# A seven-product form, used twice, for the last tile's up stage

## The chip, the cores and the metric

The kernel runs on one core of a Trainium2 chip. Its time is the device time of one execution in microseconds, the median of several runs. A core has five engines that run their own instruction queues and wait for each other through semaphores: PE (matmuls), DVE (vector work), ACT (activations, copies), POOL (element-wise work, no access to PSUM) and SP (here only a queue that issues DMA transfers). PE reads its operands from SBUF, the on-chip memory, and leaves results in banks of PSUM; a bank holds 512 float32 values in each of 128 partitions.

## What is computed

A retention layer over 8 batches, 8 heads, 576 positions and a head size of 64 makes `x`, 4608 tokens of 512 features. A gated feed-forward block follows; it is the larger part of the work and the one that the change touches. All is float32.

```python
def _moe_ref(x, w_gate, w_val, w_out) -> np.ndarray:
    g = x @ w_gate
    silu = g * (1.0 / (1.0 + np.exp(-g)))
    val = x @ w_val
    return (silu * val @ w_out).astype(np.float32)
...
    x = np.ascontiguousarray(attn_out.transpose(0, 2, 1, 3)).reshape(B * S, H * D)
    return _moe_ref(x=x, **moe_kwargs)
```

`w_gate` and `w_val` are 512 by 1536, `w_out` is 1536 by 512.

## The kernel before

**Tiles.** The tokens go in five tiles: tile 0 has 512 tokens and plain matmuls, tiles 1 to 4 have 1024 each. Each of these has an up stage (gate and value products, then Silu and a multiply) and a down stage (product with `w_out`). While tile n is computed, the retention layer for tile n+1 runs in pieces between its steps (`tick`); for tile 4 all of it is done within tile 3's stages.

**Fewer products.** The matrices of a stage are cut into blocks, and a fast scheme (the tables `UP` and `DOWN`, 26 lines each) makes the block results from 26 products of sums of blocks, where the plain form would need 32. A line of `UP` gives the label of a PSUM bank, whether the product opens the bank or adds onto what is there, the slot of the input sum with the sums that make it, the slot of the weight sum with its sums, and what is done with the product. The 1536 hidden columns are taken as three quads (`qd`, `NQ = 3`) of four 128-row blocks, gate and value side by side. So an up stage has 3 x 26 = 78 steps (`up_step`), each with four matmul calls of 128 by 128 by 256 (line 1124); a down stage has 26 steps (`down_step`) with six (line 1173). A step's products are used by `reads`: ACT copies a bank (line 1058), DVE adds bank and SBUF, POOL adds two SBUF tiles (line 1061), ACT applies Silu (line 1145) and DVE or POOL multiplies (lines 1148, 1152).

**Sums of weights.** They do not depend on the tile. They are made once: for the up stage during tile 1 (POOL and ACT), where each operand that PE uses is also written to DRAM (`up_ops`, by ACT's DMA queue), and for the down stage during tile 0 (`dn_ops`). From tile 2 on a step's operand is one load from DRAM, issued by SP, into a ring of eight slots of 768 columns (`fetch`, line 1022; `operand`). `fetch` is called after each step and loads what is needed eight steps on. The loads of the retention inputs (lines 306 to 317) and the stores of results (line 1182) go through the same SP queue, in program order.

**Sums of inputs.** A tile's input sums (`x_sums`, line 910) are made on DVE in the last steps of the down stage before it and on POOL during its first quad; the sums of hidden blocks for a down stage (also line 910) on DVE and POOL within its steps.

**Order.** The program order of each engine's queue is that of the source; `merge` spreads the retention pieces evenly over the steps of a stage. Nothing reorders it later. The instructions of an engine run in that order, each when its semaphores allow.

Of the kernel before, what the change touches and what calls it, by code (L numbers as in the profile page):

```python
# [12 lines left out]
F32 = mybir.dt.float32  # L13
# [4 lines left out]
ALU = mybir.AluOpType  # L18
# [117 lines left out]

def terms(text):

    return [t.split() for t in text.split(",") if t.strip()]
# [16 lines left out]
def kernel(  # L156
# [83 lines left out]
    ring = arena[:, 4 * QW + 2560 - 8 * 768 :].rearrange("p (s x) -> p s x", x=768)  # L240
# [672 lines left out]
    dn_ops = [dr.tile([P, 768], F32, name=f"dn{i}") for i in range(N)]  # L913

# [96 lines left out]
    fetches = [("dn", 1, i) for i in range(N)]  # L1011
    for n in range(2, NTILE):
        fetches += [("up", qd, i) for qd in range(NQ) for i in range(N)] + [("dn", n, i) for i in range(N)]
    fetched = [0]
    turn = [5, 4, 1, 6, 7, 2, 0, 3]

    def fetch():
        m = fetched[0]
        if m < len(fetches):
            what, a, i = fetches[m]  # L1020
            src = up_ops[a][i] if what == "up" else dn_ops[i]
            nc.sync.dma_start(out=ring[:, turn[m % 8], 0 : src.shape[-1]], in_=src)
            fetched[0] += 1

    used = [0]

    def operand():
        m = used[0]
        used[0] += 1
        return ring[:, turn[m % 8]]  # L1030
# [77 lines left out]
    def up_step(n, qd, i):  # L1108
# [5 lines left out]
        if busy:  # L1114
            if i > 1:
                w_sums(qd, i)
            w = up_view(qd)(wslot)
        else:
            w = operand()[:, 0:512].rearrange("p (g x) -> p g x", g=2)
# [7 lines left out]
        if busy:  # L1127
            nc.scalar.dma_start(out=up_ops[qd][i].rearrange("p (g x) -> p g x", g=2), in_=w)
            if i in (20, 23) and qd + 1 < NQ:
                first_sums(qd + 1, *((0, 2) if i == 20 else (2, 4)))  # L1130
# [5 lines left out]
            if qd + 1 == NQ:  # L1136
                for _ in range({21: 3, 22: 2, N - 1: 3}.get(i, 0)):
                    fetch()
# [23 lines left out]
    def down_step(n, i):  # L1162
        label, opens, slot, hops, ops = down[i]
        for op in hops:
            add(nc.gpsimd if i % 3 == 1 and op[0] != "nad" else nc.vector, op, hid_view)
        w = operand().rearrange("p (q x) -> p q x", q=NQ)
# [30 lines left out]
        if 0 <= at < X_FIRST and n + 1 < NTILE:  # L1197
            x_sums(n + 1, at, at + 2, True)
        go_on(3)


# [91 lines left out]
    for n in range(1, NTILE):  # L1293
        upto = needed(n + 1) if n + 1 < NTILE else done
        cut = (done + upto + (n == 1) * 2) // 2
        ups = [lambda qd=qd, i=i: up_step(n, qd, i) for qd in range(NQ) for i in range(N)]
# [49 lines left out]
```

## Time and profile before

| what | value |
|---|---|
| median of 3 runs | 1044.39 us (1042.32 to 1045.34) |
| span of the profiled execution, first to last instruction | 1037.2 us, 21564 instructions |
| mean clock granted to PE | 0.998 |
| busy in the last tile's up stage, 831.5 to 966.2 (134.7 us) | PE 134.7, DVE 56.8, ACT 34.4, POOL 49.7 |
| busy in the down stage before it, 762 to 831 (69 us) | PE 68.9, DVE 44.3, ACT 6.3, POOL 26.4 |
| busy in tile 3's up stage, 629 to 762 (133 us) | PE 133.0, DVE 62.0, ACT 33.7, POOL 45.0 |
| DMA over the span | 199.12 MB, 192 GB/s |
| operand loads of up stages | 234, 256 KB each, 2.6 us from issue to landing (median) |
| operand loads of down stages | 104, 384 KB each, 3.8 us |

The profile comes from one execution and has its own span, which begins with the first instruction and ends with the last; the device time of a run has more around it. Busy times of different engines overlap. An engine that is busy all the time sets the length of a stage; one that isn't can still do so, where another waits for it. A matmul call of float32 shows as two records of 128 by 256.

### The profile page before, as it was taken

To read this page: it belongs to the slowest core of one execution; us is meant where nothing else is said; L and a number is where in the kernel's file an instruction comes from. 1 tells how busy PE (TensorE), PEld (TensorE's weight loads), DVE (VectorE), ACT (ScalarE), POOL (GpSimd) and SP (SyncE) were. 2 spreads that over 40 slices of the span, in tenths; PEclk is the share of its full clock that TensorE was granted. 3 is DMA by queue.
4 is the path that set the end of the run, shared out by engine and by line. 5 is a ranking of instruction groups with operands and counts; after the bars stand their busy time and mean duration, and the time that the engine had idled before them with its cause. 6 is when DMAs were issued, how large, how long until landed. Compare 5 with 4: busy or idle time off the path is not lost.

```text
span 1037.2 us, 21564 instructions
## 1 busy us (share of the span) xinstructions
PE 1023.1 (99%) x8440; PEld 846.0 (82%) x8440; DVE 633.2 (61%) x1070; ACT 299.6 (29%) x653; POOL 419.9 (40%) x369
## 2 busy tenths in 40 slices
PE   6999999999999999999999999999999999999998
PEld 5654555888888888888888888888888888888887
DVE  4488878676768667446458685435465644344644
ACT  3566433253544222222322103223211022231110
POOL 3401265867564236522134057222242583222425
PEclk9999999999999999999999999999999999999999
DMA  9999877777679887674686686555554465555653
GB/s 240 258 279 263 200 218 269 204 205 191 196 194 265 211 244 220 177 197 133 188 231 173 176 208 208 153 142 153 159 171 148 143 196 153 153 153 160 182 163 100
DMA packets 307244, 199.12 MB, mean 192 GB/s; under 512 B 215944, under 2 KB 251784, under 8 KB 307144
## 3 DMA queue, kind: packets, MB, share of 16 engines
q1 hardware_dynamic: 275720, 161.17, 58.2%
q10 hardware_dynamic: 30784, 36.18, 10.4%
q8 instruction: 67, 1.10, 0.5%
q0 software_dynamic: 640, 0.39, 0.2%
q14 instruction: 33, 0.27, 0.1%
HBM read 157.58 MB, written 40.11 MB: 191 GB/s over the span
## 4 chain that ended last, share of the span: by engine, by line
PE 93%; DMA 3%; DVE 1%; ACT 1%; issue 1%; SPq 1%; POOL 0%; DVEq 0%; ACTq 0%; POOLq 0%
PE bankC L1124 13%; PE bankE L1124 13%; PE bankB L1124 13%; PE bankA L1124 13%; PE bankB L1173 7%; PE bankC L1173 7%; PE bankE L1173 7%; PE bankA L1173 7%; PE outer L556 2%; PE bankA L877 2%; PE bankB L877 1%; PE bankE L877 1%; PE outer L583 1%; PE inner L597 1%; PE inner L567 1%; PE bankC L877 1%
## 5 line engine op out<-in xcount | busy, mean ns | idle before, releaser
L1061 POOL TENSOR_TENSOR rest<-rest 128x512 f32<-128x512 f32 x65 | 91.7, 1415 | 234.3 <-DVE rest L1061 212.8
L1145 ACT ACTIVATE io<-rest 128x256 f32<-128x256 f32 x180 | 75.0, 416 | 305.4 <-DVE rest L1061 262.4
L1124 PE MATMUL bankC<-rest,arena 128*128 128x256 f32 x544 | 129.0, 380 | 0.0
L1124 PE MATMUL bankA<-rest,arena 128*128 128x256 f32 x544 | 128.7, 379 | 0.0
L910 POOL TENSOR_TENSOR arena<-arena 128x512 f32<-128x512 f32 (+1 forms) x72 | 110.6, 1549 | 37.3 <-DMA up<-arena 26.5
L1124 PE MATMUL bankB<-rest,arena 128*128 128x256 f32 x512 | 121.2, 380 | 0.5 <-DMA arena<-up 0.5
L1124 PE MATMUL bankE<-rest,arena 128*128 128x256 f32 x512 | 121.4, 380 | 0.1
L1152 POOL TENSOR_TENSOR arena<-rest,io 128x256 f32<-128x256 f32 x72 | 51.9, 726 | 167.7 <-ACT io L1145 167.7
L1124 PEld LDWEIGHTS bankA<-rest,arena 128*128 128x128 f32 x544 | 103.2, 190 | 14.5 <-issue 0.5
L1124 PEld LDWEIGHTS bankC<-rest,arena 128*128 128x128 f32 x544 | 102.9, 190 | 14.4 <-POOL arena L910 0.3
L1124 PEld LDWEIGHTS bankB<-rest,arena 128*128 128x128 f32 x512 | 97.0, 190 | 14.0 <-issue 0.8
L1124 PEld LDWEIGHTS bankE<-rest,arena 128*128 128x128 f32 x512 | 97.0, 190 | 13.7 <-DVE rest L1061 0.5
L910 POOL TENSOR_TENSOR rest<-rest 128x256 f32<-128x256 f32 (+1 forms) x69 | 68.9, 1020 | 71.8 <-DMA dn<-rest 35.3
L1061 DVE TENSOR_TENSOR rest<-bankB,rest 128x512 f32<-128x512 f32 x72 | 48.9, 687 | 67.1 <-PE bankB L1124 52.5
L1061 DVE TENSOR_TENSOR rest<-bankC,rest 128x512 f32<-128x512 f32 x72 | 48.9, 687 | 65.5 <-PE bankC L1124 46.9
L1061 DVE TENSOR_TENSOR rest<-bankA,rest 128x512 f32<-128x512 f32 x72 | 48.9, 687 | 61.2 <-PE bankA L1124 45.1
L1061 DVE TENSOR_TENSOR rest<-bankE,rest 128x512 f32<-128x512 f32 x71 | 48.2, 687 | 60.5 <-PE bankE L1124 47.1
L1148 DVE SCALAR_TENSOR_TENSOR arena<-rest,io 128x256 f32<-128x256 f32 x84 | 56.7, 676 | 10.8 <-ACT io L1145 10.8
L1173 PE MATMUL bankC<-arena 128*128 128x256 f32 x252 | 58.3, 380 | 0.1
L1173 PE MATMUL bankB<-arena 128*128 128x256 f32 x252 | 58.2, 381 | 0.0
L1173 PE MATMUL bankA<-arena 128*128 128x256 f32 x252 | 57.9, 379 | 0.0
L1173 PE MATMUL bankE<-arena 128*128 128x256 f32 x252 | 57.9, 379 | 0.0
(204 smaller groups left out, 1626.1 us busy)
## 6 DMA issues: line engine op xcount, KB each, us to landing
arena<-up SPq DMA_DIRECT2D x234, 256.0 KB, 2.6
arena<-dn SPq DMA_DIRECT2D x104, 384.0 KB, 3.8
up<-arena ACTq DMA_DIRECT2D x78, 256.0 KB, 3.7
dn<-rest SPq DMA_DIRECT2D x78, 128.0 KB, 1.8
out_dram<-rest SPq DMA_DIRECT2D x31, 256.0 KB, 3.9
qk<-in_q_dram SPq DMA_DIRECT2D x108, 72.0 KB, 2.6
qk<-in_k_dram SPq DMA_DIRECT2D x108, 72.0 KB, 2.7
rest<-in_moe_w_out_dram ACTq DMA_DIRECT2D x6, 1024.0 KB
```

The lines of the kernel that those rows point to most:

```text
L556: m = nc.tensor.matmul(value(i, hl, c), s["v"][rows, at], ret[rows, c % 2 if whole(i) else hl, c // 2], start=start, stop=start, skip_grou ...
L567: nc.tensor.matmul(z[half[hl], r, c], s["kn"][chunk(i, hl, 2 * c + r)], s["v"][rows, at], start=True, stop=True, skip_group_check=True)
L583: nc.tensor.matmul(xr[half[hl]] if c + 1 == NC else value(i, hl, c), state[half[hl], c, :], s["qT"][half[hl], ts(c, L)], start=False, stop ...
L597: nc.tensor.matmul(sc[chunk(i, hl, 2 * c + r)[0], r if whole(i) else hl, c], kT[half[hl], at], qT[half[hl], at], start=True, stop=True, sk ...
L877: nc.tensor.matmul(bank, w, xs[0][:, c, :], start=(c == 0), stop=(c == HP - 1))
L910: eng.tensor_tensor(out=dst, in0=srcs[0], in1=srcs[1], op=ALU.add if op[0] == "add" else ALU.subtract)
L1061: eng.tensor_tensor(out=at(op[1]), in0=at(op[2]), in1=at(op[3]), op=ALU.add if op[0] == "add" else ALU.subtract)
L1124: m = nc.tensor.matmul(b[:, gv * TB : (gv + 1) * TB], w[:, gv, ts(c, P)], rhs[:, c, :], start=(opens and gv == 0 and c == 0), stop=(c == 1 ...
L1145: nc.scalar.activation(out=s, in_=src[:, 0:TB], func=AF.Silu, scale=-1.0 if negative else 1.0)
L1148: return lambda: nc.vector.scalar_tensor_tensor(out=dst, in0=src[:, TB : 2 * TB], scalar=-1.0, in1=s, op0=ALU.mult, op1=ALU.mult)
L1152: nc.gpsimd.tensor_tensor(out=dst, in0=src[:, TB : 2 * TB], in1=s, op=ALU.mult)
L1173: nc.tensor.matmul(b[:, m * TB : (m + 1) * TB], lhs[:, qd, ts(m, P)], w[:, qd], start=(opens and qd == 0 and m == 0), stop=(qd == NQ - 1), ...
```

## The change

Only tile 4's up stage (`FINE = (4,)`) gets another scheme; tiles 1 to 3 keep `UP`. The product of a 2 by 2 block matrix by another is made from seven products and sums (the form with four sums on each side and seven afterwards). It is applied twice: seven outer products, in the order `FINE_ORDER = (1, 2, 6, 7, 4, 5, 3)`, each of which is itself made from seven inner products. An inner product is two matmul calls (gate and value), 128 by 128 by 256. With three quads there are 3 x 7 = 21 turns of seven inner products.

```python
        def product(k, i):
            ...
            b = bank_of(k, i)
            opens = i in (1, 2, 5)
            for g in range(2):
                nc.tensor.matmul(b[:, g * TB : (g + 1) * TB], w[:, g], x(o, i),
                                 start=(opens and g == 0), stop=True, skip_group_check=True)
```

Inner products 1, 6, 7 and 4 add onto each other in one bank (of four that take turns, `chain_banks`), and ACT copies what is there after each of the first three; 5 and 3 share a second bank, 2 has a third. The order within a turn, with what is issued to ACT and DVE, is written out. `k` is the turn, `r` the place in it; the fourth product of turn k-1 comes in turn k:

```python
        def step(k, r):
            own, last = 0 <= k < K, 0 < k
            t = temps(k)
            if own and r == 0:
                product(k, 1)
                nc.scalar.copy(out=t["p1"], in_=bank_of(k, 1))
            if own and r == 1:
                product(k, 5)
                nc.scalar.copy(out=t["p5"], in_=bank_of(k, 5))
            if last and r == 2:
                product(k - 1, 4)
                used[0] += 1
                fetch()
            if own and r == 3:
                product(k, 6)
                nc.scalar.copy(out=t["u2"], in_=bank_of(k, 6))
            if own and r == 4:
                product(k, 2)
            if own and r == 5:
                product(k, 3)
            if own and r == 6:
                product(k, 7)
                nc.scalar.copy(out=t["u3"], in_=bank_of(k, 7))
            if late and own:
                for _ in range(2):
                    if late:
                        late.pop(0)()
            if r == 0 and last:
                done(k - 1, 12)
            if r == 1 and last:
                before = temps(k - 1)
                made(k - 1, 22, before["u3"], before["p5"])
                done(k - 1, 22)
            if r == 2 and last:
                if seq[k - 1][1] == 1:
                    nc.scalar.copy(out=held[spot[21]], in_=bank_of(k - 1, 4))
                else:
                    onto(k - 1, 21, bank_of(k - 1, 4))
            if r == 3 and last:
                done(k - 1, 21)
            if own and r == 4:
                made(k, 11, bank_of(k, 2), t["p1"])
            if own and r == 5:
                made(k, 12, bank_of(k, 3), t["u2"])
            if own and r == 6:
                done(k, 11)
```

`made` is one DVE sum of 128 by 512 for one of the four inner results (11, 12, 21, 22), with one input from PSUM for 11 and 12; the result 21 is what stands in the chain's bank after product 4. `onto` adds the result to the running outer sums, also on DVE, and `finish` (called by `done` for the outer products 2, 4, 5 and 3, after which a hidden block is complete) is a Silu on ACT and a multiply on POOL:

```python
        def onto(k, c, src):

            o = seq[k][1]
            r, at = held[spot[c]], temps(k)[home[c]]
            if o == 2 or o == 3:
                combine(nc.vector, at, src, r, 1)
            elif o == 6:
                combine(nc.vector, r, src, r, 1)
            elif o == 7:
                combine(nc.vector, kept(k, c), src, r, 1)
            elif o == 4:
                combine(nc.vector, at, src, kept(k, c), 1)
            elif o == 5:
                combine(nc.vector, r, src, r, 1)
                combine(nc.vector, at, src, kept(k, c), 1)
```

The temporaries are three sets that take turns; `kept` lies in the hidden rows of the next quad. In outer product 1 `made` writes the running sums themselves, and there is no `onto`.

**Sums of inputs.** For tile 4 four outer sums of 128 by 1024 go to DVE in steps 18 to 21 of tile 3's down stage, in place of eight of 128 by 512 in steps 21 to 24; the inner sums of 128 by 256 are on POOL: 8 for outer products 1 and 2 in steps 21 to 24, 20 more (`late`) two at each place from the first turn on.

**Sums of weights.** Their 49 combinations for each quad are made in six rounds, one for each quad and side (gate or value), from eight blocks of 128 by 256. Five of the blocks are in `up_ops` already; the other three are written to DRAM by ACT's queue during tile 1's up stage (`w_raw`, after steps 2, 6 and 10 of each quad). A round loads eight blocks with SP, turns the sign of one on ACT, makes four outer sums of 128 by 512, eight inner sums of 128 by 256 and four of 128 by 384, and stores the results to `fine_ops` in DRAM with 14 or 15 transfers on SP. The rounds lie here (stage, quad, side; V is DVE, G is POOL):

```python
        def up_round(n, stage, qd, g, at):
            load, turned, outer, z4, z3, store4, store3 = weight_round(qd, g, place_up(stage), (G, V, G) if stage else (V, V, V))
            for d, blocks in enumerate(((4, 6), (0, 2), (5, 7), (1, 3))):
                put(n, stage, at + d, lambda blocks=blocks: load(*blocks))
            put(n, stage, at + 6, turned)
            ...
            put(n, stage, at + 16, lambda: store4(0))
            put(n, stage, at + 18, lambda: store4(1))
            ...
            put(n, stage, at + 22, store3)

        def down_round(n, qd, g):
            load, turned, outer, z4, z3, store4, store3 = weight_round(qd, g, place_down(), (G, G, G))
            put(n, "down", 0, lambda: load(4, 6, 0, 2))
            put(n, "down", 1, lambda: load(5, 7, 1, 3))
            ...

        down_round(1, 0, 0)
        up_round(2, 0, 0, 1, 0)
        up_round(2, 1, 1, 0, 1)
        down_round(2, 1, 1)
        up_round(3, 0, 2, 0, 0)
        up_round(3, 1, 2, 1, 1)
```

What a round is given for a step is issued ahead of that step's matmuls.

**Loads.** A turn needs all its 7 x 2 weight blocks, one load of 896 KB into one of three places of 1792 columns that share the ring's memory; there are 21. `fetch` now issues in program order whatever fits beside what is loaded and not yet used, and the ring's slots in the down stages before and in tile 4 are numbered so that the first three of these loads can go after steps 20, 22 and 24 of tile 3's down stage:

```python
    def fetch():
        while fetched[0] < len(fetches):
            lo, width = fetches[fetched[0]][3:]
            if any(f[3] < lo + width and lo < f[3] + f[4] for f in fetches[used[0] : fetched[0]]):
                return
            fetch_one()
```

The loop at the end of the kernel takes the new stage for tile 4:

```diff
-        ups = [lambda qd=qd, i=i: up_step(n, qd, i) for qd in range(NQ) for i in range(N)]
+        ups = fine_up(n) if n in FINE else [lambda qd=qd, i=i: up_step(n, qd, i) for qd in range(NQ) for i in range(N)]
```

## The prediction

> **What bounds the kernel now.** I read the page first: the busy shares, then the chain of waits that ended last.
>
> ```profile
> PE 1023.1 (99%) x8440; PEld 846.0 (82%) x8440; DVE 633.2 (61%) x1070; ACT 299.6 (29%) x653; POOL 419.9 (40%) x369
> PE 93%; DMA 3%; DVE 1%; ACT 1%; issue 1%; SPq 1%; POOL 0%; DVEq 0%; ACTq 0%; POOLq 0%
> ```
>
> PE is busy 99% and is 93% of the chain: a matmul removed is time gained, and whatever makes PE wait is time lost, one for one. Then the timeline of PE in the last tile's up stage, for the price of a step, and the stages as windows:
>
> ```profile
> 905.63 1.89 PE L1124 MATMUL bankE<-rest,arena 128*128 128x256 f32 x8
> 907.36 1.89 PE L1124 MATMUL bankB<-rest,arena 128*128 128x256 f32 x8
> ...
> 831.50:966.20 134.70, 134.70 (x626) 118.58 (x625) 56.83 (x88) 34.41 (x74) 49.69 (x49) 1.00 0.59 165
> ```
>
> Steps start 1.726 us apart. A step is four matmul calls of the program (eight records), so a call is 0.4314 us. The window (columns: length, then busy us of PE, weight load, DVE, ACT, POOL, clock, DMA share, GB/s) shows the stage that is replaced: 78 steps, 134.7 us, PE never idle, DVE busy 42%. Last, the rows that price what is put in its place: sums on DVE beside POOL (timelines of both), copies on ACT, and SP's queue.
>
> ```profile
> 908.16 0.41 DVE L1148 SCALAR_TENSOR_TENSOR arena<-rest,io 128x256 f32<-128x256 f32 x1
> 911.12 1.24 DVE L1148 SCALAR_TENSOR_TENSOR arena<-rest,io 128x256 f32<-128x256 f32 x1 [0.17 <-ACT io L1145]
> 910.65 1.42 POOL L1061 TENSOR_TENSOR rest<-rest 128x512 f32<-128x512 f32 x1 [3.02 <-DVE rest L1061]
> 923.10 1.07 ACT L1058 COPY rest<-bankC 128x512 f32<-128x512 f32 x2 [0.53 <-PE bankC L1124]
> L910 DVE TENSOR_TENSOR rest<-rest x10: 675/958/1754, 789.0 to 992.7; 128x512 f32<-128x512 f32 x8, 128x768 f32<-128x768 f32 x2
> L1061 DVE TENSOR_TENSOR rest<-bankB,rest x41: 652/691/693, 614.4 to 1029.1; 128x512 f32<-128x512 f32 x41
> ```
>
> A DVE operation with both inputs in SBUF takes 0.41 us alone and 1.24 us beside a POOL operation: it ended 0.29 us after POOL's (912.36 against 912.07). At 128x512 the minimum is 0.675 us and the maximum 1.754. With one input in PSUM it takes 0.65 to 0.69 whatever POOL does. So each POOL operation can hold up one two-SBUF sum of DVE.
>
> **What the change takes away.** 78 steps of 4 calls, 312, become 3 x 7 x 7 products of 2 calls, 294: 18 x 0.4314 = 7.77 us less PE. An inner product lasts 0.863 us, a turn (one outer product, seven inner) 6.04 us. The banks are the same size and the matmuls have the same shape, so their price stays.
>
> **What it adds in that stage.** Per group of hidden rows DVE gets 21 sums with a PSUM input and 28 with two SBUF inputs, POOL 16 multiplies (0.73 us), ACT 28 copies and 16 Silus (0.42 us). Independent DVE sums start 0.61 us apart, a sum that needs the one before it 0.72 us later; a copy's result is there after 0.59 us, and copies start 0.49 apart. The sums of a group fit (49 x about 0.65 = 32 of 42.3 us). Queue order is the trouble: ACT has the Silu of the last turn ahead of the copy that PE waits for, and the Silu waits for DVE.
>
> Turn 5, the sixth of seven, has 11 sums (the others 3 or 7). From its start, with no POOL in the way: made 11 starts at 4.56 (five products, plus 0.20 until the result is readable, as ACT's 923.10 follows PE), its two sums at 5.28 and 5.89, made 12 at 6.50, its two at 7.22 and 7.83, made 22 at 8.44, its two at 9.16 and 9.77, ending at 10.44. Silu ends at 10.9, the copy of turn 3's second chain value at 11.5. PE wants to write on in that bank at 6.04 + 6 x 0.863 = 11.22: 0.3 us late. POOL's multiplies (one left from turn 4, two of turn 5) fall between these back-to-back sums; two of them cost 0.55 each, the first 0.1: 1.3 us late. If each blocks for its whole 0.73, 1.8. I take 1.3, because DVE has no gap there into which a multiply could go. Three times: 4.0 (0.9 to 5.4).
>
> The same delay carried into the next group's first turn (7 sums of turn 3 behind the late ones) makes PE late by 0.6 (0 to 0.9) twice: 1.2. At the end nothing stands between the last group's last two products of one bank: PE waits for a copy, 0.16 + 0.04 + 0.59 + 0.05 = 0.84. The first down step lasts 2.59 us, the second wants bankA, which DVE's last sum still reads: 1.2 (0 to 1.4). At the start bankC is read by DVE until 0.1 us after PE wants it, and the 20 POOL sums of the inputs (0.73 each, about 20 us) slow turn 2's sums: 0.2. Together 0.3 (0.1 to 1.3). Sum: 4.0 + 1.2 + 0.84 + 1.2 + 0.3 = 7.5 us, from 1.8 to 10.8.
>
> The Trainium skill, page "SBUF — State Buffer", section "Who interferes with whom", says that the second of two such operations blocks fully until the first ends, and that issue order decides. The row differs a little: 0.29 us after POOL's end, not a full 0.41. By the rule turn 5 would be 1.8 late instead of 1.3, and the sum 9.0.
>
> **What it adds earlier.** Six weight rounds: each 8 loads of 128 KB and 14 stores on SP, about 4.2 MB. ACT gets 9 more copies to DRAM in tile 1's up stage (78 of them there now). A down round is 16 POOL sums, 4 x 1.27 + 8 x 0.73 + 4 x about 1.0 = 15 us, beside a POOL that is busy 26.4 of 69 us in such a stage; an up round is 16 sums on DVE, or 8 there and 8 on POOL, 8 to 10 us, beside a DVE busy 62 of 133 us. These waits go to slack that banks and the eight ring slots give: a down step's operand is fetched eight steps, 20 us, ahead. That cover is thinnest on SP in tile 2's up stage:
>
> ```profile
> 457.29 32.14 SPq L1022 DMA_DIRECT2D arena<-up  x22
> ...
> PE bankB L1124 <- DMA arena<-up: 0.5, 1, 0.5
> ```
>
> After the attention loads (450.09 to 457.29) the first fetch goes out at 457.29, lands 2.6 us later by its row and is wanted at 462.30: 2.4 us of slack. There the second up round puts two loads ahead of each of four fetches. PE has waited for such a fetch once already (0.5 us, at 426.5). Issues were 0.49 us apart in the attention loads and 0.97 in the quickest run of fetches (12 in 11.60 us). At 0.5 three issues fit in a step; at 0.97 they take 2.91 against 1.73, 4.7 us over four steps, 2.3 beyond the slack; if the fetch lands after 3.97 us, as the one issued at 422.86 did, 3.7 beyond it. The stores may add 0.6 and POOL's late sums in a down stage 0.5. So 0 to 4.8 us; I take 1.0, nearer the attention loads, because the round's loads are small like them.
>
> The new operand loads are 896 KB, 21 in place of 78 of 256 KB, issued when a slot is free: 9.5 us before use, three slots in rotation, the first three already in the last six down steps. 256 KB land in 2.6 us and 384 KB in 3.8, so 1.2 per 128 KB gives 8.6 us; by the 345 GB/s of the busiest window, 2.7. Both fit; I cost them at nothing, and PE covers them.
>
> The page "DMA: Bandwidth & Descriptors", section "Anatomy of one DMA — SWDGE (gpsimd) path", gives 2.0 us plus the bytes at 436 GB/s, for loads issued by another engine; an estimate of 4.1 us here, between the two, and the sum would not change.
>
> **Sum.** 1037.2 - 7.77 + 7.5 + 1.0 = 1037.9 us of span, +0.7. The median of the runs, 1044.4, lies 7.2 above the profiled span; I let that difference stand: 1045.1. For this kernel 0.3% is 3.1 us, about what its measurement tells from no change, so the forecast is no change.
>
> **The rivals.** *DVE's sums slip past POOL* (chance 0.30, faster): the stalls are near their lower bounds, 1.8 to 3.6 us, and nothing is lost earlier: -7.77 + 2.7 = -5.1, 1039.3 us. For it: DVE is busy 32 of 42.3 us only, and a multiply beside a PSUM sum costs nothing. Against: turn 5 has seven two-SBUF sums in eight running.
>
> *SP runs out of lead* (0.20, slower): the round's three issues a step take over 0.575 us each (a third of 1.726); from there the slack shrinks, and PE waits in tile 2's second quad once it is gone. At 0.97 and 3.97 the earlier cost is 4.8 instead of 1.0: +0.7 + 3.8 = +4.5, 1048.9. For it: the wait at 426.5 and DMA shares of 0.9 near it. Against: eight slots refill within a few steps.
>
> *The last stage's stalls are near their upper bound* (0.12, slower): 10.8 instead of 7.5, +4.0, 1048.4; the rule's reading of a blocked sum speaks for it, the multiplies that meet PSUM sums against.
>
> *The 896 KB loads land late* (0.04, slower): beyond 9.5 us every turn from the fourth waits; at 10.0 it is 18 x 0.5 = 9 us, 1052 us. The DMA share of 0.59 in that stage speaks against it.
>
> **How the numbers follow.** Forecast 0.34; faster 0.30; the three slower ones 0.20 + 0.12 + 0.04. The forecast's own range is 1041.3 to 1047.5. Lower end: -7.77 + 1.8 = -5.9, 1038.5. Upper: -7.77 + 10.8 + 4.8 = +7.8, 1052.2, but both ends at once are unlikely; I stop at +6.4, 1050.8, and leave about one in ten outside on each side. Faster 0.30, same 0.34, slower 0.36.
>
> **What would show it.** The last up stage should last 126.8 + about 5 us, with PE waiting for ACT's copies in the turn after each turn 5, 1.3 us, and 0.84 at its end; two-SBUF sums of DVE there should average well above 0.675 us. In tile 2's up stage PE's waits for fetches show the 1.0. PE without such waits makes it faster; PE waiting on "arena<-up" or "arena<-fine" for more than a few us makes it slower.

## The result: slower, and the profile after

The changed kernel takes 1080.9 us (median of four runs, 1078.8 to 1085.0), the kernel before 1044.7 beside it: a ratio of 1.037, with a 95% interval from 1.034 to 1.041. The forecast was 1045.1 with a range up to 1050.8, so it was wrong by 36 us. The profiled execution of the changed kernel has a span of 1078.6 us, against 1037.2: 41 us apart, and not 36, because the profiled execution of the kernel before was quicker than its median run.

The first two lines of the page that the prediction began with, now of the kernel after:

```profile
PE 1029.7 (95%) x8404; PEld 838.7 (78%) x8404; DVE 729.0 (68%) x1174; ACT 332.3 (31%) x719; POOL 499.0 (46%) x446
PE 72%; DMA 10%; DVE 9%; SPq 3%; issue 2%; ACT 2%; POOL 1%; ACTq 0%; DVEq 0%; POOLq 0%
```

PE has 36 records fewer and is nevertheless 7 us longer busy, and its share of the chain fell from 93% to 72%: DMA and DVE now end waits of PE. Where, the windows of the stages show (length, then busy us of PE, weight load, DVE, ACT, POOL, granted clock, DMA share, GB/s). First the kernel before, tile 3's up stage, tile 2's up stage, tile 1's down stage:

```profile
622.65:762.23 139.58, 139.58 (x901) 122.77 (x897) 67.97 (x117) 36.97 (x81) 51.34 (x51) 1.00 0.58 167
400.30:545.50 145.20, 144.74 (x1174) 126.89 (x1168) 76.13 (x144) 39.31 (x87) 49.74 (x49) 1.00 0.67 188
320.55:400.30 79.75, 79.64 (x993) 69.70 (x991) 59.69 (x89) 19.83 (x56) 28.87 (x17) 1.00 0.88 236
```

Then the kernel after, the last up stage ahead of the same three:

```profile
847.80:1005.80 158.00, 136.97 (x589) 111.54 (x589) 108.41 (x145) 65.35 (x132) 58.13 (x71) 0.98 0.41 131
634.30:778.70 144.40, 140.77 (x903) 122.56 (x897) 85.85 (x141) 37.59 (x83) 63.37 (x59) 1.00 0.72 219
403.80:557.20 153.40, 146.12 (x1175) 126.58 (x1169) 96.77 (x170) 39.83 (x89) 64.40 (x60) 1.00 0.84 247
321.20:403.80 82.60, 80.83 (x993) 69.66 (x991) 60.57 (x87) 20.16 (x57) 46.74 (x32) 1.00 0.93 254
```

The last up stage went from 134.7 to 158.0 us, although its 294 calls need only 126.8: 31 us of delay. The three earlier stages lost 2.8, 8.2 and 4.8 us. Tile 2's and tile 3's down stages did not change (77.1 and 69.2 us). These four make 39 of the 41 us between the two spans; the last down stage has 1.1 more.

**The last up stage.** PE's products there, from its timeline (start, length, and in brackets the wait ahead of it and what released it):

```profile
856.75 1.03 PE L1459 MATMUL outer<-rest,arena 128*128 128x256 f32 x4
858.71 1.10 PE L1459 MATMUL outer<-rest,arena 128*128 128x256 f32 x4 [0.93 <-DVE rest L1254]
...
867.39 1.13 PE L1459 MATMUL inner<-rest,arena 128*128 128x256 f32 x4 [0.67 <-ACT v L1522]
...
871.71 1.10 PE L1459 MATMUL inner<-rest,arena 128*128 128x256 f32 x4 [1.32 <-DVE rest L1254]
...
877.28 1.03 PE L1459 MATMUL bankC<-rest,arena 128*128 128x256 f32 x4
878.14 1.03 PE L1459 MATMUL inner<-rest,arena 128*128 128x256 f32 x4
```

Products on bankA, bankC and bankE start 0.863 us after the one ahead of them, but for two on bankA at the very end of the stage. Those on `outer` and `inner` wait. DVE's and ACT's timelines name the readers:

```profile
857.87 0.69 DVE L1254 TENSOR_TENSOR rest<-outer,rest 128x512 f32<-128x512 f32 x1 [2.96 <-PE outer L1459]
...
866.76 0.58 ACT L1522 COPY v<-inner 128x512 f32<-128x512 f32 x1 [1.69 <-PE inner L1459]
```

At 857.87 DVE reads the result of product 2, which `other_banks[2 * (k % 2) + (i == 2)]` puts into `outer[:, 1]`. Product 3 goes into `outer[:, 0]`, another bank, and still starts only when that read is done. In the same way ACT's copy at 866.76 reads `inner[:, 0]`, turn 2's chain, and holds up turn 3's first product, into `inner[:, 1]`. `inner` and `outer` are one PSUM tile of two banks each, used by the attention; the new stage takes their halves for separate banks. Summed over the stage, products into `outer` start 12.9 us late (11 times) and into `inner` 11.5 us (11 times); what would be late on separate banks too is in these sums.

One more piece is slow matmuls, not waits:

```profile
948.76 2.08 PE L1459 MATMUL outer<-rest,arena 128*128 128x256 f32 x4 [2.27 <-DVE rest L1254]
950.63 1.91 PE L1459 MATMUL bankB<-x_odd,arena 128*128 128x256 f32 x4
952.34 1.91 PE L1459 MATMUL inner<-rest,arena 128*128 128x256 f32 x4
954.04 1.39 PE L1459 MATMUL bankC<-rest,arena 128*128 128x256 f32 x4
955.27 1.03 PE L1459 MATMUL bankB<-x_odd,arena 128*128 128x256 f32 x4
```

After waits of 0.70 and 2.27 us a product took 1.7 to 1.9 us instead of 0.863, until 955; the window from 947.95 to 954.78 has a granted clock of 0.50. That is another 3.1 us.

**The earlier stages.** SP's queue at the start of tile 2's up stage and in the middle of its third quad, kernel after (start, length, and how many issues stand in the row):

```profile
388.53 0.42 SPq L1299 DMA_DIRECT2D fine<-rest  x1
389.00 4.89 SPq L1302 DMA_DIRECT2D fine<-rest  x4
...
396.29 3.58 SPq L310 DMA_DIRECT2D qk<-in_q_dram  x4
...
407.67 0.39 SPq L1228 DMA_DIRECT2D out_dram<-rest  x1
...
500.50 1.95 SPq L310 DMA_DIRECT2D qk<-in_q_dram  x4
...
508.02 0.38 SPq L1299 DMA_DIRECT2D fine<-arena  x1
508.45 3.03 SPq L1302 DMA_DIRECT2D fine<-arena  x3
511.57 6.81 SPq L1055 DMA_DIRECT2D arena<-up  x9
```

In the kernel before, the same attention load began at 386.43 and the result store after it went out at 395.10. Here they are 9.9 and 12.6 us later, because the first down stage's round has put 23 issues into this queue ahead of them. Two engines want to write over what those stores still read, and have to wait. PE waits too: for fetches, which stand behind the attention load, and at 414.54 for 0.72 us for one of ACT's late copies:

```profile
395.29 1.42 DVE L914 TENSOR_TENSOR rest<-rest 128x512 f32<-128x512 f32 x2 [4.91 <-DMA fine<-rest]
...
413.42 1.07 ACT L1096 COPY rest<-bankB 128x512 f32<-128x512 f32 x2 [8.23 <-DMA out_dram<-rest]
...
410.13 1.97 PE L1165 MATMUL bankE<-rest,arena 128*128 128x256 f32 x8 [2.59 <-DMA arena<-up]
...
511.52 1.97 PE L1165 MATMUL bankA<-rest,arena 128*128 128x256 f32 x8 [0.77 <-DMA arena<-up]
516.06 1.97 PE L1165 MATMUL bankC<-rest,arena 128*128 128x256 f32 x8 [2.58 <-DMA arena<-up]
```

The same places in the kernel before, where neither DVE nor ACT waits for a transfer:

```profile
386.43 2.17 SPq L306 DMA_DIRECT2D qk<-in_q_dram  x4
395.10 0.39 SPq L1182 DMA_DIRECT2D out_dram<-rest  x1
...
388.51 1.41 DVE L910 TENSOR_TENSOR rest<-rest 128x512 f32<-128x512 f32 x2
...
402.37 1.07 ACT L1058 COPY rest<-bankB 128x512 f32<-128x512 f32 x2 [0.67 <-PE bankB L1124]
```

At 500 to 511 PE simply runs out of operands fetched ahead: thirteen issues for the attention, one fetch, four stores, 11 us in which one operand was fetched, while PE uses one every 1.73 us.

### The profile page after: what moved, and what is told of

It reads as the page before. It is cut to its first block, busy times and chain, and to the rows that moved or that the text cites. A ratio compares the mean times of both kernels' runs of the same rounds, so it can differ in the third digit from the quotient of the medians.

```text
span 1078.6 us, 21854 instructions
## 1 busy us (share of the span) xinstructions
PE 1029.7 (95%) x8404; PEld 838.7 (78%) x8404; DVE 729.0 (68%) x1174; ACT 332.3 (31%) x719; POOL 499.0 (46%) x446
## 4 chain that ended last, share of the span: by engine, by line
PE 72%; DMA 10%; DVE 9%; SPq 3%; issue 2%; ACT 2%; POOL 1%; ACTq 0%; DVEq 0%; POOLq 0%
PE bankC L1165 8%; PE bankB L1165 8%; PE bankE L1165 8%; PE bankA L1165 7%; PE bankA L1219 6%; PE bankC L1219 6%; PE bankB L1219 6%; PE bankE L1219 5%; DVE rest L1254 3%; PE inner L1459 3%; PE outer L1459 2%; DVE rest L1099 2%; DMA v<-in_v_dram 2%; PE bankA L1459 1%; PE bankC L1459 1%
## 5 line engine op out<-in xcount | busy, mean ns | idle before, releaser
L1189 ACT ACTIVATE io<-rest 128x256 f32<-128x256 f32 x135 | 56.2, 416 | 216.7 <-DVE rest L1099 187.3
L1165 PE MATMUL bankC<-rest,arena 128*128 128x256 f32 x392 | 93.5, 382 | 3.7 <-DMA arena<-up 2.6
L1165 PE MATMUL bankA<-rest,arena 128*128 128x256 f32 x376 | 89.4, 381 | 2.1 <-DVE rest L1099 1.4
L1165 PE MATMUL bankE<-rest,arena 128*128 128x256 f32 x360 | 85.5, 380 | 2.6 <-DMA arena<-up 2.6
L1165 PE MATMUL bankB<-rest,arena 128*128 128x256 f32 x360 | 85.6, 381 | 1.3 <-ACT rest L1096 0.7
L1165 PEld LDWEIGHTS bankC<-rest,arena 128*128 128x128 f32 x392 | 73.9, 190 | 15.3 <-issue 2.9
L1165 PEld LDWEIGHTS bankA<-rest,arena 128*128 128x128 f32 x376 | 71.1, 190 | 13.4 <-DVE rest L1099 2.2
L1165 PEld LDWEIGHTS bankE<-rest,arena 128*128 128x128 f32 x360 | 68.2, 190 | 12.2 <-DVE inner L624 3.0
L1165 PEld LDWEIGHTS bankB<-rest,arena 128*128 128x128 f32 x360 | 68.1, 190 | 11.4 <-ACT rest L1096 1.3
L1254 POOL TENSOR_TENSOR rest<-rest 128x256 f32<-128x256 f32 (+3 forms) x44 | 48.8, 1124 | 37.1 <-DMA fine<-rest 19.1
```

Source lines behind the costliest of these rows:

```text
L1165: m = nc.tensor.matmul(b[:, gv * TB : (gv + 1) * TB], w[:, gv, ts(c, P)], rhs[:, c, :], start=(opens and gv == 0 and c == 0), stop=(c == 1 ...
L1189: nc.scalar.activation(out=s, in_=src[:, 0:TB], func=AF.Silu, scale=-1.0 if negative else 1.0)
L1254: eng.tensor_tensor(out=out, in0=a, in1=b, op=ALU.add if sign > 0 else ALU.subtract)
```

## The experiments

In all tables and texts the stages are named by tile: down 1 is tile 1's down stage. Lengths are from a stage's first matmul to the next one's, from the profiled execution; before, and the same code in two executions, they agree within 1 us or so, down 1 and up 2 under the rounds' load within 3. Down 2 is 77.1 us in every kernel. The ratio is to the kernel before on the same chip, with its 95% interval; the chips differ, so runs are compared by it (the median of the kernel before was 1041.1 us beside e1 to e4, 1040.3 beside e5 to e9, 1039.4 beside e10 to e12, 1039.9 beside e13 to e15, 1040.2 beside e16 and e17).

```
                          us     ratio  interval        down1  up2   up3  down3  up4  down4
before                                                  79.8 145.2 139.6  69.1 134.7  67.5
after                   1080.9  1.0371  1.0335-1.0407   82.6 153.4 144.3  69.2 158.0  68.6
e1  separate banks      1061.4  1.0196  1.0155-1.0237   83.2 155.4 143.0  69.1 135.3  68.6
e2  rounds alone        1059.1  1.0173  1.0140-1.0206   82.3 156.4 143.2  69.1 134.7  67.5
e3  new stage alone     1064.4  1.0225  1.0199-1.0250   81.0 145.2 139.6  69.1 156.7  68.6
e4  e3 + e1             1044.6  1.0035  1.0008-1.0061   80.1 144.7 139.6  69.2 136.0  68.5
e5  no round stores     1046.6  1.0068  1.0041-1.0095   81.4 146.6 141.9  69.2 135.3  68.6
e6  no round sums       1057.1  1.0151  1.0111-1.0191   82.2 155.9 140.6  69.1 136.2  68.2
e8  stores from ACT     1090.3  1.0469  1.0430-1.0508   99.2 167.3 144.3  69.1 135.3  68.6
e9  stores from POOL    1070.7  1.0293  1.0265-1.0320   83.8 158.0 153.8  69.2 135.3  68.6
e10 stores spread       1058.1  1.0170  1.0140-1.0200   83.3 153.2 143.8  69.2 136.3  68.2
e11 small stores        1049.7  1.0091  1.0065-1.0117   81.8 149.4 141.9  69.1 135.4  68.6
e12 Silu later          1052.9  1.0129  1.0079-1.0179   80.9 156.5 144.0  69.2 130.8  68.6
e13 rounds one later    1048.6  1.0076  1.0048-1.0105   80.2 152.1 143.0  69.9 131.6  68.1
e14 e13 + spread        1047.7  1.0059  1.0037-1.0082   80.0 147.4 146.0  69.8 129.3  72.0
e15 e14 + sums on DVE   1049.2  1.0087  1.0059-1.0114   79.7 149.3 144.7  69.9 128.3  72.1
e16 spread in up only   1045.8  1.0044  1.0027-1.0060   79.6 147.6 142.0  69.9 130.7  68.6
e17 heavy turn earlier  1043.2  1.0025  1.0006-1.0044   81.4 146.8 142.7  69.9 129.1  67.5
```

**Taking the two halves apart.** e1 gives the last up stage four tiles of one bank in place of the halves:

```diff
-        chain_banks = [banks[0], banks[1], inner[:, 0], inner[:, 1]]
-        other_banks = [banks[2], banks[3], outer[:, 0], outer[:, 1]]
+        ps_two.__exit__(None, None, None)
+        ps_one = ctx.enter_context(tc.tile_pool(name="ps_one", bufs=1, space=PSUM))
+        single = [ps_one.tile([P, 512], F32, name=f"single{i}") for i in range(4)]
+        chain_banks = [banks[0], banks[1], single[0], single[1]]
+        other_banks = [banks[2], banks[3], single[2], single[3]]
```

(`ps_two` is a pool of its own for `inner` and `outer`, closed here.)

> The changed kernel, with the last up stage's four banks that were halves of two two-bank tiles (inner, outer) as four tiles of one bank each; same instructions in the same order. Theory 'shared tile': of the 31.2 us in which the PE stood in that stage (158.0 long, 126.8 of matmuls), some 22 are waits for a reader of the other half of a two-bank tile, so the stage falls to about 136 us (130 to 142) and the total from 1080.9 to about 1059 (1053 to 1065). Rival 'late readers': VectorE's sums, 0.98 to 1.23 us beside GpSimd, are late for any bank; the stage stays at 155 or more and the total at 1077 or more. Under both the earlier stages stay as in the changed kernel.

e2 keeps the rounds and gives tile 4 the old stage:

```diff
-FINE = (4,)
+FINE = ()
```

> The changed kernel, but tile 4 runs the up stage of before (sums of x in its down stage, fetches of 256 KB operands); the weight rounds with their loads, sums and stores stay. Theory 'rounds': what tiles 1 to 3 lost (first down stage 2.8, second up stage 8.2, third 4.8 us) comes from the rounds' DMA issues and sums, so these stages stay as long as in the changed kernel and the total is about 1061 (1057 to 1064), with the last up stage at 134.7. Rival 'new fetches': the loss comes from the fetch order around the fine stage; then tiles 1 to 3 go back to before and the total is under 1048.

e3 is the other half, `plan_rounds()` and the writes to `w_raw` removed, and e4 is e3 with e1's tiles:

```diff
-    plan_rounds()
...
-            src = fine_ops[a].rearrange("p (g s x) -> p g s x", g=2, s=7)[:, :, i]
+            src = stand_in.rearrange("p (g s x) -> p g s x", g=2, s=7)[:, :, i]
```

> The changed kernel without the weight rounds and the three extra stores a quarter: the last tile multiplies by 896 KB loads of the same form taken from an input, so its weight sums are left out of the computation. Theory 'rounds' and 'shared tile': tiles 1 to 3 within 2 us of before, the last up stage still 158 us (155 to 161), total about 1069 (1065 to 1072). Rival 'backlog': part of the last stage's stalls is work left over from the rounds; then the stage is under 150 and the total under 1062.

> The two edits together: no weight rounds (the last tile's weight sums are left out of the computation), and four one-bank tiles in the last up stage. Theory 'shared tile': the stage is about 136 us (130 to 142) against 134.7 before, and the total 1047 (1041 to 1053): the form itself then neither gains nor loses much, as 7.8 us of matmuls are given back to waits for operands. Rival 'late readers': the stage stays at 155 or more and the total at 1066 or more.

All four came out as the theories said, but for e3's total, 0.6 us below its range. Separate tiles take the last up stage from 158.0 to 135.3 us (e1) and from 156.7 to 136.0 (e4), so the rival of late readers falls: the same sums by the same engines, as long as before (DVE busy 108.4 and 109.1 us), no longer stop PE. The rounds alone cost 17 us in down 1, up 2 and up 3, and without them these stages are back to within about 1 us. The two parts hardly touch each other. e4 also shows what the form is worth here by itself: with separate banks, and with no weight sums to pay for, its last up stage is 136.0 us against 134.7 and the whole 0.35% slower than before (0.08 to 0.61), because the delay left in the stage, 9.2 us, is more than the 7.8 us of matmuls saved. What e1's stage still has over 126.8:

```profile
847.70:983.10 135.40, 129.44 (x590) 110.85 (x589) 109.08 (x145) 65.00 (x132) 57.87 (x71) 1.00 0.47 153
```

```profile
890.56 1.13 PE L1464 MATMUL single<-x_odd,arena 128*128 128x256 f32 x4 [1.39 <-ACT rest L1520]
...
897.34 1.13 PE L1464 MATMUL single<-rest,arena 128*128 128x256 f32 x4 [0.47 <-ACT rest L1520]
```

The copy that PE waits for stands behind a Silu in ACT's queue, and the Silu behind a sum of DVE (ACT's timeline of e1):

```profile
889.62 0.42 ACT L1475 ACTIVATE io<-v 128x256 f32<-128x256 f32 x1 [1.69 <-DVE v L1256]
889.94 0.57 ACT L1520 COPY rest<-single 128x512 f32<-128x512 f32 x1
```

This comes after each turn of eleven sums, and is what the prediction had described.

**What of the rounds costs.** All from e1 on; the edits are shown in part, and the rounds in down stages are changed alike. e5 leaves out their stores, e6 their sums:

```diff
-            put(n, stage, at + 16, lambda: store4(0))
-            put(n, stage, at + 18, lambda: store4(1))
...
-            put(n, stage, at + 22, store3)
```

> Four one-bank tiles as in e1, and the weight rounds without their stores (13 or 14 issues and 3.2 MB each); loads and sums of the rounds stay, and the last tile reads its 896 KB operands from an input, so its weight sums are left out of the computation. In e1 the first down stage is 83.2 us, the second up stage 155.4, the third 143.0: 17 over before. Theory 'queue' (SyncE's queue issues the rounds' stores in a row ahead of fetches and result stores): the three lose at most 5 us together, total about 1047 (1043 to 1050). Rival 'bandwidth' (DMA busy share 0.92 and 0.83 there): the same, as the bytes go too. Rival 'sums' (VectorE and GpSimd): the loss stays above 11 us, total above 1054.

```diff
-            put(n, stage, at + 6, turned)
-            for d, f in enumerate(outer):
-                put(n, stage, at + 7 + d, f)
...
```

> As e1, but the rounds' sums are left out: their loads and stores move the blocks as they are, so the last tile's weight sums are left out of the computation. Theories 'queue' and 'bandwidth': the three stages still lose 12 us or more, total 1056 or more. Rival 'sums': they lose less than 5 us, total 1048 or less.

Without stores the three stages are 5.3 us over before, without sums 14.1, with both 17.0. So the stores carry the larger part; what leaving out the sums gained is mostly the 2.4 us in up 3. e8 and e9 ask whether it is SP's queue or the traffic, by issuing the stores elsewhere:

```diff
-                nc.sync.dma_start(out=to[:, 2 * n + k, 0:512].rearrange("p (m x) -> p m x", m=2), in_=quarter(n, k))
+                nc.scalar.dma_start(out=to[:, 2 * n + k, 0:512].rearrange("p (m x) -> p m x", m=2), in_=quarter(n, k))
```

(and the other three kinds of store; `nc.gpsimd` in e9).

> As e1, with the rounds' stores issued by ScalarE instead of SyncE; the same bytes and the same sums. Theory 'queue': the three stages lose at most 7 us instead of 17, total about 1049 (1045 to 1054); ScalarE's own copies may wait up to 2 us behind a store that waits for its sum. Rival 'bandwidth': nothing moves, the loss stays at 14 us or more and the total at 1058 or more.

> As e1, with the rounds' stores issued by GpSimd, which makes nearly all of the sums, instead of SyncE. Theory 'queue': as with ScalarE, at most 7 us lost, total about 1049 (1045 to 1054), unless GpSimd's own time for an issue delays its sums. Rival 'bandwidth': the loss stays at 14 us or more, total 1058 or more.

The totals, 1090.3 and 1070.7, are far from the 1049 of 'queue'. By the letter they lie in the rival's "1058 or more", but the rival said that nothing would move, and against e1 both became slower. They do not tell queue from traffic, because each made a new wait. ACT's timeline in e8, and PE's row after it:

```profile
361.09 0.90 ACTq L1296 DMA_DIRECT2D fine<-rest  x2
...
375.42 0.58 ACT L1098 COPY rest<-bankA 128x512 f32<-128x512 f32 x1 [19.19 <-DMA qk<-in_q_dram]
...
371.01 4.38 PE L1221 MATMUL bankA<-arena 128*128 128x256 f32 x12 [9.83 <-DMA arena<-dn]
```

ACT has a store next at 356.2 and issues it at 361.1, while POOL makes the sums that it takes (from 358.2 on); ACT's later work stands behind it. SP's next attention load is held for 9.3 us, by its row for "DMA fine<-rest", with the fetches behind it, and PE for 9.8. Why that load has to wait for these stores was not tried. In e9 a store costs POOL itself 0.72 us (POOL's timeline: 3 in 2.16):

```profile
445.67 2.16 POOL L1298 DMA_DIRECT2D fine<-arena  x3
447.86 1.27 POOL L1101 TENSOR_TENSOR rest<-rest 128x512 f32<-128x512 f32 x1
```

POOL, with these issues, is busy 81.7 us in up 2 instead of 64.0 in e1, its sums come late, and PE waits 5.7 us there for the sums of DVE that follow them, and 8.7 us in up 3. The Trainium skill, page "DMA: Bandwidth & Descriptors", section "Issuing engines are not separate DMA queues", says that transfers from any engine run on the same 16 DMA engines and that another issuer saves only the time to issue. Nothing here speaks against that, and the runs add that the issuer's own queue can lose more than that time (ACT stood for 19.2 us in e8).

e10 leaves them on SP, at most two in a step; e11 keeps the places and cuts each store to 16 of 128 partitions:

```diff
-            put(n, stage, at + 16, lambda: store4(0))
-            put(n, stage, at + 18, lambda: store4(1))
+            for d, f in enumerate(store4(0) + store4(1)):
+                put(n, stage, at + 14 + d // 2, f)
```

> As e1, with the rounds' stores still from SyncE, but at most two in a step (two of the first ten from two steps earlier on, the last three or four one in a step) where four or five stood in a row; each step's own fetch comes between. Theory 'order' (a row of stores behind an attention load of 11 issues keeps SyncE from fetching for 11 us, with a lead of some 14 us of which 4 to 5 are the landing): the second up stage loses at most 5 us instead of 10.2, the third at most 3, the first down stage keeps its 3; total about 1055 (1050 to 1058). Rival 'bandwidth': nothing moves; 1059 or more.

> As e1, with every store of the rounds cut to 16 of its 128 partitions: the same number of issues at the same places, an eighth of the bytes; the last tile reads its operands from an input, so its weight sums are left out of the computation. Theory 'order' in its strict form (the number of issues, 0.4 us each at least): the three stages still lose 11 us or more, total 1055 or more. Rival 'bandwidth' (what has to be moved makes issues long and landings late): they lose 7 us or less, as without stores; total 1050 or less.

e10 gained some 3 us, fewer than expected, and less than the two intervals can tell. In up 2's third quad PE's wait for fetches is 0.9 us instead of 3.7 in e1, but a wait of 3.9 us stayed at the start of the stage, where DVE waits 6.9 us for "DMA fine<-rest". In e11 the three stages are 8.5 us over before instead of 17.0, between the two theories; its total, 1049.7, is the rival's. Small stores are issued quicker (the three after the attention load in 1.35 us, against 3.03 in the kernel after) at unchanged places, so their size counts for half of the loss. That their number counts too is not shown: e11 is 3.2 us over e5, which has no stores, about as much as executions of one code differ there. (The expectation of e10 gives the attention load 11 issues; the rows show thirteen.)

**Silu out of the way.** e12 is e1 with `finish` five products later, except in the last two turns:

```diff
         def done(k, c):
             if 0 <= k < K and seq[k][1] in final:
-                finish(k, c)
+                waiting.append([5 if k + 2 < K else 0, k, c])
...
         def step(k, r):
+            drain(1)
```

> As e1, with each Silu and its multiply of the last up stage put five products later (not in the last two turns), so that ScalarE's copies of the chain bank no longer stand behind a Silu that waits for VectorE's late sum. Theory 'Silu in the way': PE's waits of 1.4 to 1.5 and 0.5 us after each turn with eleven sums go, the stage falls from 135.3 to about 130 (128 to 132), total about 1056. Rival 'late sums' (VectorE, busy 109 of 135 us, is what PE waits for by way of any reader): the wait moves to VectorE's reads, the stage stays at 134 or more.

The stage fell to 130.8 us; the waits after the first two heavy turns are gone, with the same sums on DVE (busy 105.6 us). The rival falls.

**Order of the rounds.** e13 is e12 with the rounds one place on:

```diff
-        down_round(1, 0, 0)
-        up_round(2, 0, 0, 1, 0)
-        up_round(2, 1, 1, 0, 1)
-        down_round(2, 1, 1)
-        up_round(3, 0, 2, 0, 0)
-        up_round(3, 1, 2, 1, 1)
+        up_round(2, 0, 0, 0, 0)
+        up_round(2, 1, 0, 1, 1)
+        down_round(2, 1, 0)
+        up_round(3, 0, 1, 1, 0)
+        up_round(3, 1, 2, 0, 1)
+        down_round(3, 2, 1)
```

> As e12 (four one-bank tiles, Silu five products later), with the six weight rounds moved one place on: none in the first down stage, two in the second up stage, one in the second down stage, two in the third up stage, one in the third down stage, which loads nothing for the attention. Theory 'attention loads ahead' (the first down stage's round costs 1 to 3 us there and some 4 to 5 at the start of the second up stage, since its last five stores and the result stores stand behind attention loads and VectorE's sums of x wait to write over what they read): first down stage 79.8 to 80.3, second up stage 149 to 152, third down stage at most 70.5, total about 1046 (1043 to 1049). Rival 'bytes' (a round costs its 3.2 MB wherever it stands): the total stays at 1051 or more, the third down stage takes 3 us or more.

Down 1 is 80.2, up 2 152.1, down 3 69.9, and the total, 1048.6, is in the expected range and below the rival's 1051. The round of the first down stage, with the same bytes, costs 0.7 us in tile 3, and by e12's stages about 5 where it stood; that size is rough, since executions differ by up to 3 us in up 2 and the two ratios' intervals overlap. The mechanism shows in the rows: DVE waits no more for "fine<-rest", the result store goes out at 395.03, as before. What is left in up 2 is the row behind the attention load, and after a wait of 3.53 us PE is again slow (eight records in 3.75 us instead of 1.89):

```profile
508.40 3.75 PE L1167 MATMUL bankC<-rest,arena 128*128 128x256 f32 x8 [3.53 <-DMA arena<-up]
```

e14 adds e10's spreading, e15 moves the rounds' sums in up stages to DVE (`(V, V, V)`), e16 spreads in up stages only, and e17 makes the heavy turn the fifth:

> As e13, with the stores spread as in e10, and the Silu of the last turn with eleven sums moved too. Theory 'order': the late fetches in the second half of the second up stage (3.4 and 0.5 us of waits and the slow start after them) go, so the stage is 146 to 149; the last up stage falls by the 1.5 us wait at its end to about 129.3; total about 1042 (1039 to 1045), the same as the kernel before. Rival 'bytes': as e13 or within 1.5 us of it.

> As e14, with all sums of the rounds in up stages on VectorE (in the second and third quarter GpSimd made eight of sixteen). Theory: in the third up stage the 3.5 us over before are GpSimd's sums of products coming late (PE waits for copies and sums that follow them), so the stage falls to 141 or less and the total to about 1040 (1037 to 1043). Rival: VectorE, 86 of 143 us busy there, becomes late itself, and the stage stays at 143 or more.

```diff
-FINE_ORDER = (1, 2, 6, 7, 4, 5, 3)
+FINE_ORDER = (1, 2, 6, 7, 5, 4, 3)
```

> As e13, with the stores spread in the up stages only, and the Silus as in e13. From e13 and e14: second up stage 147 to 148, third 142 to 143.5, last up stage 131, last down stage 68.6, total 1044 (1041 to 1047), 3 to 4 over the kernel before. If spreading in the second down stage was not what made e14's third up stage 146.0, that stage is above 144.5.

> As e16, with the turn of eleven sums fifth instead of sixth in each quarter, so that two turns of seven follow it before the last down stage. Theory: the wait of 1.5 us that e12 kept near the end of the last up stage (and 0.9 us after it) shrinks, the stage falls to about 129.5 and the total to 1042 (1039 to 1045), the same as the kernel before within its 0.3 per cent. Rival: VectorE is behind by the same sums at the end, whatever their order; the stage and the last down stage together stay within 0.7 us of e16.

In e14 up 2 is as expected (147.4), the total not: 1047.7 instead of at most 1045. Up 3 was 146.0, and the last Silus, moved too, made down 4 start late (72.0 instead of 68.1); the second is why e16 leaves them where they were. e15 speaks against its theory: up 3 is 144.7, not 141 or less, and above the rival's 143, and the total is no better; so that POOL's sums cause the rest in up 3 is not shown, nor is what does. e16 is as expected, and its up 3 of 142.0 speaks for spreading in down 2 as what had made it 146.0. In e17 the last up and down stages together are 2.7 us shorter than in e16, against the rival. It is the best version found: 0.25% over the kernel before (0.06 to 0.44). Its last up stage is 5.6 us shorter than before, but down 1, up 2, up 3 and down 3 still lose 7.1 together, so nothing here beats that kernel. e17's stages:

```profile
324.70:406.10 81.40, 80.05 (x994) 69.95 (x992) 59.94 (x89) 19.92 (x56) 28.97 (x17) 1.00 0.89 235
406.10:552.80 146.70, 145.16 (x1169) 126.59 (x1168) 94.22 (x168) 39.81 (x89) 61.73 (x57) 1.00 0.82 243
630.00:772.60 142.60, 140.37 (x898) 122.38 (x896) 85.63 (x141) 37.59 (x83) 63.26 (x58) 1.00 0.72 220
842.50:971.60 129.10, 127.73 (x590) 111.45 (x589) 104.91 (x146) 65.22 (x133) 58.35 (x71) 1.00 0.50 160
```

Up 2 moves 243 GB/s here and loses 1.6 us; in the kernel after it moved 247 and lost 8.2. So it was the order in the queue, more than the rate of the traffic, that cost there.

## Why the prediction was wrong, point by point

- *PE saves 7.77 us.* Right: where nothing holds it up, each product starts 0.863 us after the last, as priced.
- *"The banks are the same size and the matmuls have the same shape, so their price stays."* This step failed, and it cost most: 22.7 us of the last up stage (158.0 to 135.3 in e1). Size and shape are the same, but four of the eight banks were halves of two tiles, and a product into one half waits for the reader of the other. The list of `chain_banks` and `other_banks` and the two allocations of [P, 2, 512] were both in the code; the PE timeline could not show it, as the old stage used only whole-bank tiles.
- *Stalls of 7.5 us in the new stage.* Right in place and nearly in size, once the banks are apart (e1). Delay after the heavy turn 1.63, 1.72 and 1.72 (1.3 each predicted), next turn twice 0.63 (0.6), end 0.95 (0.84), second down step 1.03 (1.2), start 0.2 (0.3). Their cause too: e12 moved the Silu and the first two were gone; how much of each is POOL's doing was not tried. The prediction's own terms for a heavy turn, 0.3 + 0.55 + 0.55 + 0.1, add up to 1.5 and not 1.3, which is nearer to what was measured.
- *Earlier stages 1.0 us, at most 4.8.* This term was mis-sized: 15.8 us in the kernel after and 17.3 in e2. The bound came from one place, loads ahead of fetches in tile 2's second quad, and that place held. Not counted were rows of four or five stores behind an attention load (3.7 of the 5.0 us that PE waits for fetches in e1's up 2), and that a store late in the queue keeps the memory it reads, so that DVE's sums of x and ACT's copies wait at the start of up 2. The prediction gave the stores 0.6. The 0.97 us between fetches, with which it made its upper bound, was no price of an issue: in the same trace three fetches are issued in 1.36 us (at 393.65).
- *The rivals.* "SP runs out of lead" named the right resource, at 4.8 us against 17.3, but in another place: PE waited at the start of tile 2's up stage and in its third quad. The stalls were not at their bounds either way. The 896 KB loads never were late: no wait of PE names them, and they land 4.9 us after their issue in e1 (median), well within 9.5.
- *Smaller slips.* The 7.2 us from span to run time were not a property of the kernel: in every later run the time is 1.7 to 2.1 us over the span, so some 5 us of the forecast came from a profiled execution that was quicker than the median run. Loads late by 0.5 us in 18 turns would have made about 1054 us, not 1052. And tile 3's up stage begins at 622.65, not at 629, so DVE is busy 68.0 of its 139.6 us.

## What to carry to other kernels

Before PSUM is given a new use, ask of what tiles its banks are parts: two banks in one tile act as one for the waits, even where instruction and bank differ. When transfers are added to a queue, count not only what stands behind them but what wants to write over the memory they read; it is cheaper to place them where the queue has no other bursts than to move them to an engine that also computes. And ahead of the copy that PE waits for, an in-order engine should have nothing that waits for a slower one.

## What was not expected of the hardware

PE can pay for a wait twice. In the kernel after, a wait of 2.27 us, with one of 0.70 shortly before it, was followed by four slow products (3.1 us lost). In e8 the wait of 9.83 was followed by 12 records in 4.38 us where 2.75 is usual, and the clock of that stage was 0.91. In e13 3.53 us had the same effect. A wait of 2.59 us at 410.13 in the kernel after did not, nor one of 3.39 in e12, although one of 2.77 in e12 did. The Trainium skill, page "TensorE: Matmul & The Clock Gate", section "HAM oscillation — how this bites in real kernels", gives idle gaps over some 3.4 us as what throttles the clock. The longest waits agree with that; the 2.27 and the 2.77 do not.

The profiles show what decides. Within one execution the stretches at half clock begin whole multiples of 3.413 us apart: in e6 at 410.44, 516.26 (31 times) and 980.47 (136 times after that). On that grid, e12 (length, then busy us of PE, weight load, DVE, ACT, POOL, granted clock, DMA share, GB/s):

```profile
406.28:409.69 3.41, 1.22 (x6) 1.12 (x7) 3.05 (x9) 0.00 (x0) 3.33 (x3) 1.00 0.99 320
409.69:413.10 3.41, 3.41 (x10) 2.69 (x9) 0.00 (x0) 1.07 (x2) 0.36 (x1) 0.50 1.08 385
...
512.09:515.50 3.41, 1.84 (x8) 1.28 (x8) 0.69 (x1) 0.00 (x0) 0.62 (x1) 1.00 1.08 338
515.50:518.92 3.42, 1.60 (x8) 1.44 (x8) 0.00 (x0) 0.42 (x1) 1.36 (x2) 1.00 0.98 292
```

The wait of 2.77 us lies in one stretch and leaves PE busy 1.22 of 3.41 us (0.36): half clock follows. The longer wait, 3.39, is split over two, each with PE busy about half of the time, and nothing follows. From 165 us on, in all 18 profiles of this case, half clock begins after every full-clock stretch of the grid in which PE was busy at most 0.41 of the time, and after no other but one with 0.48 (e13, 968.26 to 971.67); eight more with 0.46 to 0.49 were not followed by it. So a wait that is shorter than the grid's step costs more or less by where it happens to fall, and two executions of the same code can differ by it: the waits of 1.46 and 0.68 us at the end of the last up stage were followed by half clock in e6 and e10, not in e1.
